# Batch 0 of a fused attention and SwiGLU kernel: turns before scores, idle PSUM banks, and copies split between two engines

## Chip, cores, metric

One core of one Trainium2 chip. The metric is the device time of one execution in microseconds (us); lower is better. Times below are medians of several executions.

## The reference, cut to what matters

Eight batches. Per batch and head: k and v are projected along the sequence by E and F, scores are taken against the projected k, softmax, times the projected v. The result is the input of a gated feed-forward network.

```python
k_proj = np.einsum('ks,bhsd->bhkd', E, k)            # 1024 -> 64 positions
v_proj = np.einsum('ks,bhsd->bhkd', F, v)
scores = scale * np.matmul(q, k_proj.transpose(0, 1, 3, 2))
attn = softmax(scores)                               # max, exp, sum, divide
x = np.matmul(attn, v_proj)                          # then heads side by side
out = (silu(x @ w_gate) * (x @ w_val)) @ w_out       # (8192, 512) x (512, 1536) twice, then back
```

## The kernel before

The main loop runs 192 feature tiles of the feed-forward part, and hides the attention of later batches between them. It cannot start before the first half of batch 0 has gone through attention. This is the stage that the change touches. The pieces, with cuts marked:

```python
ps_g = ... bufs=2   # PSUM: gate        ps_v = ... bufs=2   # value
ps_y = ... bufs=1   # output            ps_a = ... bufs=3   # attention

def u_T(b, u):            # a turn: four transposes of q, then a copy to SBUF
    ps = ps_a.tile([P, 4, P], BF16, name="qTp", tag="pa")
    ...                                      # 4 x nc.tensor.transpose
    nc.scalar.copy(out=t[:], in_=ps[:])
def u_S(b, u):            # scores of one unit, then exp
    ps = ps_a.tile([P, 4, P], FP32, name="sc", tag="pa")
    ...                                      # 4 x nc.tensor.matmul with BD, the projected k
    nc.scalar.activation(out=e, in_=ps, func=AF.Exp, scale=scale)
# u_R: sum and reciprocal on VectorE; u_N: divide (AA); u_A: turn AA, copy to AT;
# u_PV: AT times the projected v (BDV), copy to xT; u_KV: project k or v; u_KT: turn k into BD

turn(0); warm(6)                             # E turned; dummy matmuls that keep TensorE busy
cast_k(nc.vector, 0); cast_k(nc.scalar, 1); cast_k(nc.vector, 2); cast_k(nc.gpsimd, 3)
...                                          # loads of q, v and the first weights
u_KV(0, "k", (0, 4))
cast_k(nc.scalar, 4); cast_k(nc.vector, 5); cast_k(nc.vector, 6); cast_k(nc.scalar, 7)
u_KV(0, "k", (4, 8)); turn(1); u_KT(0)
for u in range(4):
    u_T(0, u); u_S(0, u)
    if u == 1: warm(2)
for u in range(4):
    u_R(0, u); u_N(0, u)
u_A(0, 0); u_A(0, 1); warm(4); u_KV(0, "v", (0, 4))
u_A(0, 2); u_A(0, 3); u_PV(0, 0, 0); u_PV(0, 0, 1); warm(4); u_KV(0, "v", (4, 8))
u_PV(0, 0, 2); u_PV(0, 0, 3)
...                                          # other loads, then the main loop
```

The softmax here doesn't subtract the row's maximum and nothing guards it: scores larger than these inputs give would overflow.

## Time and profile before

| | before |
|---|---|
| median, range of the first 3 runs | 611.54 us, 611.24 to 613.02 us |
| profiled execution | 610.9 us, span on the core 608.7 us |
| TensorE busy | 586.6 us, 96% |
| last quarter of k cast from | 10.56 us |
| fourth exp of batch 0 ends | 22.83 us |
| fourth gate matmul ("start point") | 32.56 us |

Three views matter. The *chain of waits* goes back from the last instruction and names what released each step. The *timeline* has for each group its start, its length, its engine and line, and in brackets how long the engine had been idle and what ended that. The *table by windows* gives busy times and the granted clock per stretch. A group's length tells the clock too: in the traces here eight k or v matmuls of 256 columns took 1.03 to 1.06 us at full clock and 1.86 to 1.92 us at half; four warming matmuls of 512 columns 1.02 to 1.03 and 1.86 to 1.91 us.

### The profile page before, as it was taken

Reading aid. Unit: us, or ns where it says so; the run is one execution under the profiler, and the core shown is the slowest. Engines: PE = TensorE matmul, PEld = TensorE weight load, DVE = VectorE, ACT = ScalarE, POOL = GpSimd, SP = SyncE. Lnnn points to the kernel's source line nnn. Section 1 sums busy time; section 2 is a strip of 40 time slices with the busy share of each in tenths; the row PEclk is TensorE's granted clock in tenths of the full one; section 3 lists DMA queues with packets and bytes.
Section 4 is the critical chain, followed back from the end, with each engine's and each line's share of the span. In section 5 each row is a group of like instructions: output and inputs, shape, how many; then the busy total and the mean of one; then the engine's idle time right before and its main releaser. Section 6 shows DMA issues by size and latency. Waiting matters only on the chain.

```text
span 608.7 us, 8650 instructions
## 1 busy us (share of the span) xinstructions
PE 586.6 (96%) x3279; PEld 289.6 (48%) x3344; DVE 355.7 (58%) x622; ACT 267.0 (44%) x479; POOL 105.7 (17%) x118
## 2 busy tenths in 40 slices
PE   5799999999999999999999999999999999999996
PEld 3444444545544455444544455444554455444443
DVE  3467564756655666556656666656665666655550
ACT  3336344554544445353453445354453544433231
POOL 5615030211300122011310113101220111100000
PEclk9699999999999999999999999999999999999999
DMA  9998963000940039100690009500192000000002
GB/s 227 171 198 136 195 111 70 35 20 34 177 85 34 36 52 206 38 24 28 111 168 18 35 36 154 107 36 36 33 208 56 17 36 36 34 20 36 34 36 86
DMA packets 50681, 48.79 MB, mean 80 GB/s; under 512 B 1872, under 2 KB 41296, under 8 KB 50640
## 3 DMA queue, kind: packets, MB, share of 16 engines
q0 software_dynamic: 40176, 28.84, 32.7%
q1 hardware_dynamic: 10464, 19.40, 8.7%
q8 instruction: 26, 0.43, 0.3%
q14 instruction: 15, 0.12, 0.1%
HBM read 60.29 MB, written 16.78 MB: 127 GB/s over the span
## 4 chain that ended last, share of the span: by engine, by line
PE 93%; ACT 3%; DVE 2%; issue 1%; DMA 1%; another core or an unknown queue 0%; DVEq 0%; ACTq 0%
PE yps L311 27%; PE gps L270 26%; PE vps L285 26%; PE kvp L142 3%; PE sc L201 3%; PE pv L254 2%; PE aTp L241 2%; PE qTp L187 2%; PE warm L409 1%; ACT qT L193 1%; DMA Eraw<-in_E_dram 1%; DVE hT L299 1%; ACT ee L205 0%; ACT ysb L320 0%; ACT xT L261 0%
## 5 line engine op out<-in xcount | busy, mean ns | idle before, releaser
L294 DVE SCALAR_TENSOR_TENSOR s<-th,gps 128x512 f32<-128x512 f32 x192 | 130.4, 679 | 127.9 <-ACT th L278 127.6
L270 PE MATMUL gps<-xT,wg 128*128 128x512 bf16 x761 | 196.9, 379 | 0.8 <-ACT xT L261 0.3
L311 PE MATMUL yps<-wo,hT 128*128 128x512 bf16 x760 | 193.1, 379 | 1.4 <-ACT ysb L320 0.7
L285 PE MATMUL vps<-xT,wv 128*128 128x512 bf16 x720 | 192.2, 379 | 1.9
L278 ACT ACTIVATE th<-gps 128x512 f32<-128x512 f32 x192 | 114.7, 597 | 153.7 <-PE gps L270 124.3
L299 DVE TENSOR_TENSOR hT<-s,vps 128x512 bf16<-128x512 f32 x192 | 131.9, 687 | 22.8 <-PE vps L285 2.5
L224 POOL TENSOR_TENSOR AA<-ee,rr 128x512 bf16<-128x512 f32 x62 | 64.4, 1040 | 417.2 <-DVE rr L218 281.2
L311 PEld LDWEIGHTS <-hT 128*128 128x128 bf16 x768 | 75.2, 98 | 91.4 <-issue 1.0
L270 PEld LDWEIGHTS <-wg 128*128 128x128 bf16 x768 | 72.1, 98 | 76.3 <-issue 1.0
L285 PEld LDWEIGHTS <-wv 128*128 128x128 bf16 x768 | 71.8, 98 | 77.0 <-issue 4.2
L320 ACT ACTIVATE ysb<-yps 128x512 f32<-128x512 f32 x64 | 38.2, 597 | 71.3 <-PE yps L311 68.2
L216 DVE TENSOR_REDUCE zz<-ee 128x8 f32<-128x512 f32 x64 | 43.6, 681 | 18.0 <-ACT ee L205 17.7
L205 ACT ACTIVATE ee<-sc 128x512 f32<-128x512 f32 x64 | 38.2, 596 | 33.7 <-PE sc L201 32.3
L193 ACT COPY qT<-qTp 128x512 bf16<-128x512 bf16 x64 | 37.2, 582 | 25.3 <-PE qTp L187 25.3
L261 ACT CAST xT<-pv 128x512 bf16<-128x512 f32 x64 | 36.8, 582 | 24.0 <-PE pv L254 24.0
L246 DVE COPY AT<-aTp 128x512 bf16<-128x512 bf16 x64 | 26.7, 421 | 22.5 <-PE aTp L241 21.7
L201 PE MATMUL sc<-BD,qT 128*128 128x128 bf16 x256 | 25.5, 224 | 5.2 <-ACT qT L193 4.5
L241 PEld LDWEIGHTS <-AA 128*128 128x128 bf16 x256 | 19.7, 99 | 14.7 <-POOL AA L224 0.4
L187 PEld LDWEIGHTS <-qb 128*128 128x128 bf16 x256 | 19.5, 99 | 13.2 <-issue 1.1
L187 PE MATMUL qTp<-ident_bf,qb 128*128 128x128 bf16 x256 | 25.2, 222 | 0.0
L254 PE MATMUL pv<-AT,BDV 128*128 128x512 bf16 x64 | 23.7, 379 | 1.5 <-DVE AT L246 0.8
L241 PE MATMUL aTp<-ident_bf,AA 128*128 128x128 bf16 x256 | 24.9, 222 | 0.0
(45 smaller groups left out, 175.1 us busy)
## 6 DMA issues: line engine op xcount, KB each, us to landing
out_dram<-ysb SPq DMA_DIRECT2D x64, 256.0 KB, 2.0
qb<-in_q_dram POOLq DMA_DIRECT2D x15, 512.0 KB, 9.5
kb<-in_k_dram POOLq DMA_DIRECT2D x7, 1024.0 KB, 10.7
vb<-in_v_dram POOLq DMA_DIRECT2D x7, 1024.0 KB, 12.4
kraw<-in_k_dram SPq DMA_DIRECT2D x4, 512.0 KB, 5.8
wg<-in_moe_w_gate_dram POOLq DMA_DIRECT2D x6, 256.0 KB, 10.3
wv<-in_moe_w_val_dram POOLq DMA_DIRECT2D x6, 256.0 KB, 10.9
wo<-in_moe_w_out_dram POOLq DMA_DIRECT2D x2, 768.0 KB, 15.8
```

The lines of the kernel that those rows point to most:

```text
L187: nc.tensor.transpose(out=ps[:, n, :], in_=src[:, 4 * g + n, 2 * i : 2 * i + 2, :].rearrange("p j d -> p (j d)"), identity=ident_bf[:],)
L193: nc.scalar.copy(out=t[:], in_=ps[:])
L201: nc.tensor.matmul(out=ps[:, n, :], lhsT=t[:, n, :], rhs=BD[b % 2][:, 4 * g + n, :], start=True, stop=True)
L216: nc.vector.reduce_sum(out=z[:], in_=e[:], axis=AX.X)
L224: eng.tensor_tensor(out=a[:].rearrange("p j h k -> p h j k"), in0=ee.pop((b, u))[:], in1=rr.pop((b, u))[:].unsqueeze(3).to_broadcast([P, 4 ...
L241: nc.tensor.transpose(out=ps[:, pr, j, :], in_=a[:, j, 2 * pr : 2 * pr + 2, :].rearrange("p h k -> p (h k)"), identity=ident_bf[:],)
L270: nc.tensor.matmul(out=ps[:], lhsT=wg[:, kt, f * P : (f + 1) * P], rhs=x[:, kt, :], start=(kt == 0), stop=(kt == NKT - 1),)
L278: nc.scalar.activation(out=th[:], in_=ps[:], func=AF.Tanh, scale=0.5)
L285: nc.tensor.matmul(out=ps[:], lhsT=wv[:, kt, f * P : (f + 1) * P], rhs=x[:, kt, :], start=(kt == 0), stop=(kt == NKT - 1),)
L294: nc.vector.scalar_tensor_tensor(out=s1[:], in0=th[:], scalar=1.0, in1=g[:], op0=ALU.add, op1=ALU.mult)
L299: nc.vector.tensor_tensor(out=hT[c][:, f, :], in0=s1[:], in1=ps[:], op=ALU.mult)
L311: nc.tensor.matmul(out=yy[c][:], lhsT=hT[c][:, f, i * P : (i + 1) * P], rhs=wo[:, f, :], start=(f == 0), stop=(f == NFT - 1),)
```

## The change

The intent: do all turns of q before their scores, so that TensorE does not wait for each copy (in the kernel before it idled 1.76, 0.94, 0.68 and 0.74 us for one ahead of its four score groups); take idle gate, value and output banks so that no tile waits for a bank; share the copies between ScalarE and VectorE; cast k mostly on VectorE; and run the v groups beside the divisions.

```diff
-    def u_T(b, u):
+    def u_T(b, u, at="a", eng=nc.scalar):        # likewise u_S, u_KV, u_KT (at), u_A, u_PV (eng)
...
-            nc.scalar.copy(out=bd[64:128, :, c, 64:128], in_=src)
+            copy(nc.scalar if b else nc.vector, bd[64:128, :, c, 64:128], src)
-        eng = nc.vector if b == 0 and u in (1, 3) else nc.gpsimd
+        eng = nc.vector if b == 0 and u == 3 else nc.gpsimd
...
-        warm(6)
-        cast_k(nc.vector, 0, (0, 8)) ... cast_k(nc.gpsimd, 3, (0, 8))
+        warm(4)
+        for h in range(7):
+            cast_k(nc.gpsimd if h == 3 else nc.vector, h)
...                                     # loads as before
-        u_KV(0, "k", (0, 4)); four casts; u_KV(0, "k", (4, 8)); turn(1); u_KT(0)
-        for u in range(4):
-            u_T(0, u); u_S(0, u)
-            if u == 1: warm(2)
-        for u in range(4):
-            u_R(0, u); u_N(0, u)
-        u_A 0, 1; warm(4); v group; u_A 2, 3; u_PV 0, 1; warm(4); v group; u_PV 2, 3
+        u_KV(0, "k", (0, 4), at="y"); warm(2); cast_k(nc.scalar, 7)
+        u_KV(0, "k", (4, 8), at="y"); turn(1); u_KT(0, at="v")
+        u_T(0, 0, "a", nc.scalar)
+        u_T(0, 1, "a", nc.vector)
+        u_T(0, 2, "a", nc.scalar)
+        u_S(0, 0, "g")
+        u_T(0, 3, "v", nc.vector)
+        u_S(0, 1, "g"); u_S(0, 2, "a"); u_S(0, 3, "a")
+        for u in range(3):
+            u_R(0, u); u_N(0, u)
+        u_KV(0, "v", (0, 4), at="y")
+        u_R(0, 3); u_N(0, 3)
+        u_A(0, 0, nc.scalar); warm(2); u_A(0, 1, nc.scalar)
+        u_KV(0, "v", (4, 8), at="y")
+        u_A(0, 2, nc.scalar); u_PV(0, 0, 0, nc.vector); u_PV(0, 0, 1, nc.vector)
+        u_A(0, 3, nc.scalar); u_PV(0, 0, 2, nc.scalar); u_PV(0, 0, 3, nc.vector)
```

(Several calls per line and words in place of calls are cuts. turn() and warm() also moved to value banks, and turn() copies on ScalarE only.)

More of the change, by code (lines that the diff above doesn't have):

```diff
@@ L130, with bank, copy, u_KV @@
     kvp = {}
-    def u_KV(b, what="kv", hs=(0, H)):
+    banks = {"a": (ps_a, "pa"), "g": (ps_g, "gps"), "v": (ps_v, "vps"), "y": (ps_y, "yps")}
+    def bank(where, shape, dt, name):
+        pool, tag = banks[where]
+        return pool.tile(shape, dt, name=name, tag=tag)
+    def copy(eng, out, in_):
+        (nc.scalar.copy if eng is nc.scalar else eng.tensor_copy)(out=out, in_=in_)
+    def u_KV(b, what="kv", hs=(0, H), at="a"):
         key = (b, what)
         if key not in kvp:
-            kvp[key] = ps_a.tile([P, H, D], FP32, name="kvp", tag="pa")
+            kvp[key] = bank(at, [P, H, D], FP32, "kvp")
         t = kvp[key]
@@ L159, in u_KV, with u_KT @@
             kvp.pop(key)
-    def u_KT(b):
+    def u_KT(b, at="a"):
         ks = kvp.pop((b, "s"))
-        t = ps_a.tile([P, NPAIR, KP], BF16, name="kTp", tag="pa")
+        t = bank(at, [P, NPAIR, KP], BF16, "kTp")
         for pr in range(NPAIR):
@@ L174, in u_KT @@
             nc.vector.tensor_copy(out=bd[0:64, :, c, 0:64], in_=src)
-            nc.scalar.copy(out=bd[64:128, :, c, 64:128], in_=src)
+            copy(nc.scalar if b else nc.vector, bd[64:128, :, c, 64:128], src)
     qT, ee, rr, AA, AT = {}, {}, {}, {}, {}
-    def u_T(b, u):
+    def u_T(b, u, at="a", eng=nc.scalar):
         ch, w = divmod(u, 4)
         g, i = divmod(w, 2)
-        ps = ps_a.tile([P, 4, P], BF16, name="qTp", tag="pa")
+        ps = bank(at, [P, 4, P], BF16, "qTp")
         src = qb[b, ch]
@@ L192, in u_T, with u_S @@
         t = aw.tile([P, 4, P], BF16, name="qT", tag="qT", bufs=4)
-        nc.scalar.copy(out=t[:], in_=ps[:])
+        copy(eng, t[:], ps[:])
         qT[b, u] = t
-    def u_S(b, u):
+    def u_S(b, u, at="a"):
         g = (u % 4) // 2
-        ps = ps_a.tile([P, 4, P], FP32, name="sc", tag="pa")
+        ps = bank(at, [P, 4, P], FP32, "sc")
         t = qT.pop((b, u))
@@ L230, in u_N, with u_A @@
         AA[b, u] = a
-    def u_A(b, u):
+    def u_A(b, u, eng=nc.vector):
         ch, w = divmod(u, 4)
@@ L245, in u_A, with u_PV @@
                 )
-        nc.vector.tensor_copy(
-            out=AT[b, ch][:, 2 * g : 2 * g + 2, 2 * i : 2 * i + 2, :], in_=ps[:]
-        )
-    def u_PV(b, ch, pr):
+        copy(eng, AT[b, ch][:, 2 * g : 2 * g + 2, 2 * i : 2 * i + 2, :], ps[:])
+    def u_PV(b, ch, pr, eng=nc.scalar):
         if (b, ch) not in xT:
@@ L260, in u_PV @@
         )
-        nc.scalar.copy(out=xT[b, ch][:, pr, :], in_=ps[:])
+        copy(eng, xT[b, ch][:, pr, :], ps[:])
     gp = {}
@@ L382, with cast_k @@
         new_k(0)
-        def cast_k(eng, h, js):
-            dst = kb[0][:, h, js[0] : js[1], :].rearrange("p j d -> p (j d)")
-            src = kraw[:, h, js[0] * D : js[1] * D]
-            (nc.scalar.copy if eng is nc.scalar else eng.tensor_copy)(out=dst, in_=src)
+        def cast_k(eng, h):
+            copy(eng, kb[0][:, h].rearrange("p j d -> p (j d)"), kraw[:, h])
         def turn(which):
             for half in range(2):
-                ps = ps_a.tile([P, 4, KP], FP32, name="efp", tag="pa")
+                ps = bank("v", [P, 4, KP], FP32, "efp")
                 for i in range(4):
@@ L399, in turn @@
                 js = slice(4 * half, 4 * half + 4)
-                if half == 0:
-                    nc.vector.tensor_copy(out=(ET, FT)[which][:, js, :], in_=ps[:])
-                else:
-                    nc.scalar.copy(out=(ET, FT)[which][:, js, :], in_=ps[:])
+                copy(nc.scalar, (ET, FT)[which][:, js, :], ps[:])
         def warm(n):
-            ps = ps_y.tile([P, CW], FP32, name="warm", tag="yps")
+            ps = bank("v", [P, CW], FP32, "warm")
             for _ in range(n):
@@ L415 @@
         turn(0)
-        warm(6)
-        cast_k(nc.vector, 0, (0, 8))
-        cast_k(nc.scalar, 1, (0, 8))
-        cast_k(nc.vector, 2, (0, 8))
-        cast_k(nc.gpsimd, 3, (0, 8))
+        warm(4)
+        for h in range(7):
+            cast_k(nc.gpsimd if h == 3 else nc.vector, h)
         load_q(0, 0, 2)
@@ L424 @@
         load_w_gv(1)
-        u_KV(0, "k", (0, 4))
-        cast_k(nc.scalar, 4, (0, 8))
-        cast_k(nc.vector, 5, (0, 8))
-        cast_k(nc.vector, 6, (0, 8))
-        cast_k(nc.scalar, 7, (0, 8))
-        u_KV(0, "k", (4, 8))
-        turn(1)
-        u_KT(0)
-        for u in range(4):
-            u_T(0, u)
-            u_S(0, u)
-            if u == 1:
-                warm(2)
-        for u in range(4):
+        u_KV(0, "k", (0, 4), at="y")
+        warm(2)
+        cast_k(nc.scalar, 7)
+        u_KV(0, "k", (4, 8), at="y")
+        turn(1)
+        u_KT(0, at="v")
+        u_T(0, 0, "a", nc.scalar)
[3 more added lines that the diff above has]
+        u_T(0, 3, "v", nc.vector)
+        u_S(0, 1, "g")
+        u_S(0, 2, "a")
+        u_S(0, 3, "a")
+        for u in range(3):
             u_R(0, u)
             u_N(0, u)
-        u_A(0, 0)
-        u_A(0, 1)
-        warm(4)
-        u_KV(0, "v", (0, 4))
-        u_A(0, 2)
-        u_A(0, 3)
-        u_PV(0, 0, 0)
-        u_PV(0, 0, 1)
-        warm(4)
-        u_KV(0, "v", (4, 8))
-        u_PV(0, 0, 2)
-        u_PV(0, 0, 3)
+        u_KV(0, "v", (0, 4), at="y")
+        u_R(0, 3)
+        u_N(0, 3)
+        u_A(0, 0, nc.scalar)
+        warm(2)
+        u_A(0, 1, nc.scalar)
+        u_KV(0, "v", (4, 8), at="y")
+        u_A(0, 2, nc.scalar)
+        u_PV(0, 0, 0, nc.vector)
+        u_PV(0, 0, 1, nc.vector)
+        u_A(0, 3, nc.scalar)
+        u_PV(0, 0, 2, nc.scalar)
+        u_PV(0, 0, 3, nc.vector)
         load_w_gv(2)
```

## The prediction

> **What bounds the kernel now**
>
> I read the page first (busy shares, slices, chain), then the first 33 us in the chain of waits in order of time, then the timeline of that stretch, then the landing times of the loads.
>
> ```profile
> PE 586.6 (96%) x3279; PEld 289.6 (48%) x3344; DVE 355.7 (58%) x622; ACT 267.0 (44%) x479; POOL 105.7 (17%) x118
> ...
> PE 93%; ACT 3%; DVE 2%; issue 1%; DMA 1%; another core or an unknown queue 0%; DVEq 0%; ACTq 0%
> ```
>
> TensorE is the bound, so the only time to be had lies where it waits. The change touches only work before the main loop and batch 0. The main loop begins with the first gate matmul. In the timeline:
>
> ```profile
> 31.43 1.07 ACT L261 CAST xT<-pv 128x512 bf16<-128x512 f32 x2 [2.20 <-PE pv L254]
> 31.45 1.49 PE L270 MATMUL gps<-xT,wg 128*128 128x512 bf16 x4
> ```
>
> Four xT parts feed the first gate group; the last is copied at 32.5 us, and the fourth gate matmul runs at 32.56 us (chain: "32.56 0.38 PE gps"). I call 32.56 us the start point. After it the chain is nearly all matmuls, spaced by 0.216 us. So the time saved is the distance by which the start point moves, as long as weights and later loads still land in time.
>
> The chain from 13.6 to 24.8 us goes from engine to engine instead:
>
> ```profile
> 13.62 0.29 DVE BD L174
> 13.93 0.37 ACT BD L175
> 14.33 0.30 DVE BD L174
> 14.66 0.37 ACT BD L175
> 15.05 0.59 ACT qT L193
> 15.69 0.41 PE sc L201 x4
> ...
> 19.18 0.59 ACT qT L193
> 19.82 0.62 PE sc L201 x4
> ...
> 21.06 0.48 ACT qT L193
> 21.59 0.61 PE sc L201 x4
> 22.20 0.85 PE aTp L241 x8
> 23.05 1.71 PE warm L409 x4
> 24.76 1.86 PE kvp L142 x8
> ```
>
> The reader is to see a turn of q, a copy on ACT, its scores, and only then the next turn: four rounds of about 1.8 us, since ACT also has an exp of 0.60 us in each round. Then four warming matmuls and the v projection stand in line. At 24.7 us the v data had long landed (below).
>
> Half of this stretch ran at half clock, as the table by windows shows (the third figure from the end of a row is the granted clock):
>
> ```profile
> 16.00:16.25 0.25, 0.25 (x6) 0.13 (x3) 0.00 (x0) 0.13 (x1) 0.00 (x0) 1.00 1.16 160
> 16.25:16.50 0.25, 0.06 (x2) 0.00 (x0) 0.00 (x0) 0.25 (x1) 0.00 (x0) 0.51 1.21 172
> ...
> 26.25:26.50 0.25, 0.25 (x2) 0.00 (x0) 0.00 (x0) 0.00 (x0) 0.25 (x1) 0.51 1.35 170
> 26.50:26.75 0.25, 0.25 (x5) 0.22 (x5) 0.11 (x1) 0.00 (x0) 0.25 (x1) 1.00 1.31 160
> ```
>
> The loads give the floors. Issue time plus time to landing, from the DMA view cut into short windows:
>
> ```profile
> qb<-in_q_dram POOLq DMA_DIRECT2D x1, 256.0 KB, 5.4
> ...
> vb<-in_v_dram POOLq DMA_DIRECT2D x1, 512.0 KB, 8.2
> ...
> vb<-in_v_dram POOLq DMA_DIRECT2D x1, 512.0 KB, 10.0
> ```
>
> Second half of q: issued about 9.05, landed 14.45 us. v: issued 9.88 and 10.6, landed 18.1 and 20.6 us. The first four weight pieces, issued from 11.34 with 10.6 to 12.4 us each, landed at 21.9, 23.3, 24.6 and 25.9 us.
>
> [...]
>
> [...] The trace has 0.588 us for ACT (xT); for DVE its 0.293 us (128 columns) and 0.425 us (256) make 0.69 us by a straight line, which I use. [...] the BD copies on DVE and ACT alternate and never overlap. [...]
>
> **The change part by part**
>
> *k casts.* Before, the last k matmuls started at 11.41, after two ACT casts queued behind the ks copy (10.22 to 11.36). Now only head 7 is on ACT. The last k quarter landed near 10.5 us (the DVE cast that waited for it started at 10.56), so DVE ends head 6 at 10.99 and ACT head 7 at about 11.15: start 11.2. Saved 0.2 us. [...] the second k group may then run cold, 8 x 0.213 us plus latency = 1.85 instead of 1.03 us. That would cost 0.8 us here.
>
> *BD.* Four DVE copies, 4 x 0.31 = 1.24 us, in place of 13.62 to 15.02 = 1.40. With the k gain, BD is ready at 14.65 (or 15.65 if cold) against 15.02.
>
> *Turns first.* In TensorE's order: T0, T1, T2, S0, T3, S1, S2, S3. T2 needs the second half of q, landed 14.45, almost when BD is ready, so it costs nothing. S0 at 14.75, S1 at 15.25 (qT1 copied on DVE, 0.42 us, after BD), S2 at 15.5, S3 at 15.9, done at 16.3. The bank spreading (two score tiles in the gate banks, the fourth turn in a value bank) is what lets this go without waiting for copies. ACT: qT0, qT2 until 15.45, then four exps of 0.60 us: done 16.05, 16.65, 17.25, 17.85. Before, the fourth exp ended at 22.83. So this stage is 5.0 us shorter.
>
> *Normalising.* DVE takes 0.69 + 0.20 us per unit: rr0 16.97, rr1 17.87, rr2 18.78. POOL, now three units instead of two: 17.1 to 18.2, 19.2, 20.25 us. The 0.35 us per unit that POOL is slower matters little, as the next wait is v.
>
> *v.* The first v group cannot start before 18.1. Warm: 18.1 to 19.2; cold 20.0 (1.92 us in the trace). DVE's BDV copies (2 x 0.3 us) stand before unit 3 in its queue: R3 and N3 (0.69 + 0.20 + 0.69 us) end at 21.4 warm, 22.3 cold.
>
> *The tail.* Warm: A0 19.2, A1 20.0, second v group 20.65 (landed 20.6) to 21.7, A2 22.0, BDV 22.3. AT copies on ACT 0.58 each. PV0 and PV1 at 22.0 to 22.6, their xT copies on DVE 0.69 each, 23.1 and 23.8; A3, its copy, PV2 and PV3 run beside them, PV3 done 24.2 and its xT copy at 24.9. Start point 25.0. Cold throughout (matmuls of 128 columns 0.107 us apart, of 512 0.427): A0 20.6, warming 21.3, A1 21.9, second v group 23.65, BDV 24.3, PV1 25.2, xT1 25.8, A3's copy 26.1, PV3 26.9, last xT copy 27.6. Start point 27.65.
>
> *Sum.* 32.56 - 25.0 = 7.5 us at best; 32.56 - 27.65 = 4.9 us at worst. [...] I give the warm course 0.6: 0.6 x 7.5 + 0.4 x 4.9 = 6.5 us. 611.5 - 6.5 = 605.0 us.
>
> **The rivals**
>
> *The weights take the place of the removed waits.* The loads run without a break from 8 to over 50 us (DMA share above 1 in every window), so later weights land when they did before, while the loop wants them up to 7.5 us earlier. For: the loop takes a new piece of the weights every two feature tiles, 3.45 us, and the pieces land only 2.7 us apart or more. Against: each has room. The third pair's value part (issued about 23.95, 5.4 us: 29.3) is wanted at 31.1 or later; q for the second half of the batch (26.14 + 9.5 = 35.6) at 44.86 - 7.6 = 37.2; the fifth pair's value part (27.76 + 10.6 = 38.3) at about 39.5; and k of batch 1 (33.3 + 21.8 = 55.1) at 68.7 - 7.6 = 61.1. The least margin is some 1.2 us. If this rival holds, 1 to 2 us come back: 606 to 607.
>
> *The copies become the bound.* DVE now has the BD, qT, xT copies beside the sums and BDV. [...] the BDV copies, waiting for v, hold up unit 3. For: DVE is busy nearly all of 16 to 24 us in my count. Against: the PV tail hangs on A3 only after PV1's copies. If v were 1 us later, all is 1 us later: 606.
>
> *The clock stays low into the loop.* Only 4 + 2 + 2 = 8 warming matmuls are left of 6 + 2 + 4 + 4 = 16, which gives the array less to do. [...]
>
> *Nothing of it reaches the end.* If the loop had its own slack, the gain would vanish: 611. Against: after 32.56 the chain is TensorE on TensorE.
>
> **Range and chances**
>
> 605.0 us; 8 in 10 between 603.0 and 607.3: from the warm course with the full 7.5 us (604.0) and 1 us of error in my favour, to the cold course (606.6) with 0.7 us against. Faster by over 2% needs 599.3 us, a saving of 12.2 us: the start point would have to be at 20.3, before the second half of v has landed. So faster 0.02, within 2% 0.97, slower 0.01.
>
> **What would show it**
>
> In the timeline of the changed kernel: the fourth gate matmul near 25 to 27.7 us; the four exps back to back and done by 18 to 19 us; the first v group waiting for its DMA at about 18.1 us; the second within 1 us of its landing or right behind A1; the granted clock at 1.00 from 19 us (warm course) or 0.5 until over 22 (cold). The step on the k casts is right if the second k group starts at 11.2. I am wrong if the gate or value matmuls wait for weights between 25 and 45 us, if S2 or S3 waits for a bank, or if the span falls by much less than the start point moves.

The sum came to 32.56 - 25.0 = 7.5 us warm (full clock), 32.56 - 27.65 = 4.9 us cold (half clock), and with the chances of 0.6 and 0.4 to 6.5 us, 605.0 us. The 0.6 and a cold second k group stand as estimates. The spacings at half clock (0.107, 0.213 and 0.427 us for matmuls of 128, 256 and 512 columns) are those of TensorE in the trace of before from 22.2 to 26.2 us. In the profile of before, one unit's division took 1.042 us on GpSimd and 0.691 us on VectorE; the "0.35 us per unit" is their difference. In the changed kernel's profile, VectorE ended the third unit's reciprocal at 21.48 us, then did two BDV copies at 21.52 and 21.82, and only at 22.15 the sum of the fourth unit (R3), whose exp had ended at 20.50.

## The result

| | before | changed |
|---|---|---|
| median, range (4 runs each) | 612.28 us, 611.24 to 613.18 | 605.01 us, 604.50 to 605.28 |
| ratio, 95% interval | | 0.9881, 0.9860 to 0.9902 |
| span of the profiled execution | 608.7 us | 603.5 us |
| start point | 32.56 us | 26.98 us |
| span minus start point | 576.1 us | 576.5 us |

A ratio is the mean time of one kernel's fast runs over that of the other's of the same rounds, so it is not quite the ratio of the medians. The outcome is within 2%, and 605.01 us is next to the predicted 605.0. The page's busy line, and the two lines of the timeline at the start point:

```profile
PE 584.4 (97%) x3272; PEld 288.3 (48%) x3336; DVE 356.8 (59%) x624; ACT 265.8 (44%) x476; POOL 106.7 (18%) x119
```

```profile
26.04 1.32 PE L276 MATMUL gps<-xT,wg 128*128 128x512 bf16 x4
...
26.24 0.69 DVE L138 CAST xT<-pv 128x512 bf16<-128x512 f32 x1 [0.61 <-PE pv L260]
```

The last xT copy, now on VectorE, ends at 26.24 + 0.69 = 26.93 us, and the fourth gate matmul follows at 26.98. TensorE is busy for 2.2 us less in a span that is 5.2 us shorter, so its share rises by a point. The span's 5.2 us are the start point's 5.6 us, less the 0.4 us by which the rest takes longer. That the medians differ by 7.3 us and the profiles by only 5.2 needs an explanation; it is in the next part.

The chain of waits of the changed kernel (start, length, what), where before had four rounds of copy, scores and turn:

```profile
3.00 9.35 DMA kraw<-in_k_dram
...
12.36 0.63 ACT kb L138
...
13.03 1.86 PE kvp L150 x8
...
16.36 1.40 PE qTp L195 x12
17.76 0.43 PE sc L209 x4
18.19 0.43 PE qTp L195 x4
18.62 0.29 PE sc L209 x4
...
18.93 1.09 ACT ee L213 x2
...
20.07 0.68 POOL AA L232
...
21.07 1.04 POOL AA L232
```

Turns and scores now follow one another on TensorE from 16.36 to 18.9 us, and the chain then goes through the exps and GpSimd's divisions. The four exps, which stood in four separate rounds before, now run in one stretch (ScalarE's timeline):

```profile
18.27 2.23 ACT L213 ACTIVATE ee<-sc 128x512 f32<-128x512 f32 x4
```

The first line of the chain is a load: the last quarter of k, issued at 3.00 us, on which everything after it hangs. The timeline, VectorE alone, shows when that quarter could be cast, first in before, then in the changed kernel:

```profile
10.56 0.43 DVE L387 CAST kb<-kraw 128x512 bf16<-128x512 f32 x1 [1.19 <-DMA kraw<-in_k_dram]
```

```profile
12.36 0.51 DVE L138 CAST kb<-kraw 128x512 bf16<-128x512 f32 x1 [0.22 <-DMA kraw<-in_k_dram]
```

In the changed kernel's profiled execution k landed 1.8 us later. Over the 14 profiled executions, of kernels that all issue the k loads in the same way and from 1.4 us on, this moment lay anywhere from 10.47 to 12.81 us. It is not tied to the change: before with some warming matmuls added had 12.51 us. So the profile of before was of a quick execution (610.9 us with a median of 612.3), and a fairer figure for comparing two traces is the *start point minus the cast of the last k*: 22.0 us before, 14.6 us after. That this difference, 7.4 us, is so near the 7.3 us of the medians is partly chance: in the next call the same two kernels are 9.1 us apart by the medians (8.5 us by the ratio).

One thing more differs between executions. The times of before spread from 610.0 to 613.5 us, and the mean granted clock for each execution goes with them. Later, before ran 33 times: the 11 executions with a mean clock of 0.988 to 0.992, as in the profile, took 610.0 to 611.7 us; the other 22, with 0.985 and 0.986 or with 0.999 and 1.000, took 612.3 to 613.5 us. So the profile shows the quicker of two kinds. What the slower kind does in this stage, and whether a late k goes with it, is not known, as no such execution was profiled.

### The profile page after: what moved, and what is told of

It reads as the page before. It is cut to its first block, busy times and chain, and to the rows that moved or that the text cites. A ratio compares the mean times of both kernels' runs of the same rounds, so it can differ in the third digit from the quotient of the medians.

```text
span 603.5 us, 8638 instructions
## 1 busy us (share of the span) xinstructions
PE 584.4 (97%) x3272; PEld 288.3 (48%) x3336; DVE 356.8 (59%) x624; ACT 265.8 (44%) x476; POOL 106.7 (18%) x119
## 4 chain that ended last, share of the span: by engine, by line
PE 93%; ACT 2%; DMA 2%; DVE 1%; issue 1%; SPq 0%; POOL 0%; DVEq 0%; ACTq 0%
PE yps L317 27%; PE vps L291 27%; PE gps L276 26%; PE kvp L150 3%; PE sc L209 2%; PE qTp L195 2%; PE aTp L249 2%; PE pv L260 2%; DMA kraw<-in_k_dram 2%; DVE hT L305 1%; ACT ee L213 0%; ACT qT L138 0%; DVE s L300 0%; DVE zz L224 0%; POOL AA L232 0%
## 5 line engine op out<-in xcount | busy, mean ns | idle before, releaser
L138 ACT CAST xT<-pv 128x512 bf16<-128x512 f32 x61 | 35.3, 582 | 16.9 <-PE pv L260 16.9
L138 DVE COPY AT<-aTp 128x512 bf16<-128x512 bf16 x60 | 25.2, 422 | 22.4 <-PE aTp L249 21.7
L249 PE MATMUL aTp<-ident_bf,AA 128*128 128x128 bf16 x256 | 24.8, 220 | 1.1 <-POOL AA L232 0.8
```

The lines of the kernel that those rows point to most:

```text
L138: (nc.scalar.copy if eng is nc.scalar else eng.tensor_copy)(out=out, in_=in_)
L249: nc.tensor.transpose(out=ps[:, pr, j, :], in_=a[:, j, 2 * pr : 2 * pr + 2, :].rearrange("p h k -> p (h k)"), identity=ident_bf[:],)
```

## The experiments

All were timed in five rounds against before. "k" is the start of the last VectorE cast of k, which waits for its load; "start" is the start of the fourth gate matmul. Both are read from the one profiled execution (in order_undone_filled the record of one of the four gate matmuls is missing; its last one is taken, which follows the one before it by 0.32 us as the fourth does in again). "half clock" is when the array ran at half clock in that execution, by the clock records of its trace and the lengths of the groups.

| run | median us | ratio to before, 95% | k | start | start - k | half clock, us |
|---|---|---|---|---|---|---|
| before | 612.3 to 612.8 | | 10.56 | 32.56 | 22.0 | to 9.4, 16.3-26.5 |
| changed | 605.01 | 0.9881 (0.9860-0.9902) | 12.36 | 26.98 | 14.6 | to 18.6 |
| again | 603.59 | 0.9861 (0.9841-0.9881) | 10.85 | 25.34 | 14.5 | to 12.5 |
| order_undone | 606.74 | 0.9920 (0.9898-0.9942) | 11.36 | 28.98 | 17.6 | to 13.6, 17.0-23.9 |
| tail_undone | 607.94 | 0.9916 (0.9888-0.9945) | 12.81 | 30.89 | 18.1 | to 24.7 |
| copies_undone | 607.13 | 0.9911 (0.9899-0.9923) | 11.83 | 29.05 | 17.2 | to 23.1 |
| banks_undone | 604.96 | 0.9870 (0.9854-0.9886) | 10.47 | 24.98 | 14.5 | to 11.9 |
| casts_undone | 603.75 | 0.9853 (0.9835-0.9871) | 10.77 | 25.37 | 14.6 | to 13.6 |
| order_undone_filled | 607.38 | 0.9910 (0.9893-0.9927) | 11.00 | 27.31 | 16.3 | to 12.5 |
| clock_alone | 611.55 | 0.9985 (0.9966-1.0004) | 12.51 | 34.30 | 21.8 | to 8.0, 11.4-21.7 |
| order_alone | 609.24 | 0.9946 (0.9927-0.9966) | 11.62 | 31.50 | 19.9 | to 23.0 |
| no_warm | 603.81 | 0.9864 (0.9844-0.9884) | 10.54 | 25.16 | 14.6 | to 19.4 |
| better_tail | 603.78 | 0.9860 (0.9839-0.9880) | 11.41 | 25.25 | 13.8 | to 20.1 |
| better_loads | 602.98 | 0.9852 (0.9831-0.9872) | 11.75 | 25.64 | 13.9 | to 20.1 |

In every one of these the span minus the start point is between 576.1 and 576.7 us. So the premise of the whole argument, that the main loop costs the same whenever it starts, held in all fourteen. The last column is a warning: the clock came up for good anywhere from 11.9 us (banks_undone) to 24.7 us (tail_undone) in the changed kernel and its variants, so the difference of one pair of traces holds the edit and the clock together.

Theory: the start point moves, by the order of the score rounds, the copies and the tail, with the clock adding to it. Rivals: the clock alone does it; one part alone does it; the banks or the k casts are main terms.

### again: the changed kernel once more

No edit.

> The changed kernel once more, as the reference for the others. If the saving is the movement of the start point (the fourth gate matmul), the time is 7 us below before (ratio 0.988 to 0.990), and the span minus the start point is 576 to 577 us as in both profiles seen so far. The last quarter of k landed at 10.5 us in the profile of before and at 12.36 us in that of the changed kernel: if that is chance of one execution, here it is somewhere between and the start point moves with it one for one (12.36 gave 26.98, so 10.5 would give about 25.1); if it belongs to the change, it is 12.4 again.

The median was 603.59 us, and k was early (10.85 us) with this same kernel, so its lateness in the first profile was not the change's doing. The start point followed about one for one: 25.34 us, 1.64 us earlier for 1.51 us of k. TensorE's timeline shows what stands next behind k:

```profile
18.03 1.03 PE L150 MATMUL kvp<-vb,FT 128*64 128x256 bf16 x8 [0.94 <-DMA vb<-in_v_dram]
...
20.85 1.06 PE L150 MATMUL kvp<-vb,FT 128*64 128x256 bf16 x8 [0.66 <-DMA vb<-in_v_dram]
```

Both v groups wait for v itself, 0.94 and 0.66 us. With early k the stage, up to the second v group, is at the floor that the loads set; with late k (the first profile) neither v group waits for a load. So the 14.5 and 14.6 us of start minus k come about in two ways. In the first profile the array was at half clock until 18.6 us and the exps ended 8.1 us after k; in again, at full clock, they ended after 7.2 us, and the wait for v took the 0.9 us back. That v is late when k is late has a reason in the traces: GpSimd casts one head of k before it issues the loads of q and v (cast at 7.56 and first issue at 8.37 us in again, 8.66 and 9.47 in the first profile).

### order_undone: turn, scores, turn, scores

```diff
-u_T(0, 0, "a", nc.scalar); u_T(0, 1, "a", nc.vector); u_T(0, 2, "a", nc.scalar); u_S(0, 0, "g")
-u_T(0, 3, "v", nc.vector); u_S(0, 1, "g"); u_S(0, 2, "a"); u_S(0, 3, "a")
+u_T(0, 0, "a", nc.scalar); u_S(0, 0, "g"); u_T(0, 1, "a", nc.vector); u_S(0, 1, "g")
+u_T(0, 2, "a", nc.scalar); u_S(0, 2, "a"); u_T(0, 3, "v", nc.vector); u_S(0, 3, "a")
```

In the diffs that follow T, S, R, N, A and PV with a number stand for these calls for that unit.

> The changed kernel with turns and scores alternating again (T0 S0 T1 S1 T2 S2 T3 S3), all else kept. Theory (the order is a main term): rounds of about 1.25 us (turn 0.4, copy 0.42 or 0.58, scores 0.4) in place of 0.5 us each, so the last scores end 2 us later, the first v group, which stands behind them in TensorE's queue, starts 2 us later: 606.5 to 607.5 us, ratio to before 0.991 to 0.9935. Rival (the banks and the split copies do it, the order is decoration): within 0.5 us of the changed kernel, ratio 0.988 to 0.989.

It measured 606.74 us, 3.1 us over the changed kernel run in the same call, and start minus k grew by 3.1 us. All six executions (606.1 to 609.1 us) lie above the four of again (603.0 to 604.7). The rival falls. TensorE's timeline:

```profile
17.51 0.61 PE L209 MATMUL sc<-BD,qT 128*128 128x128 bf16 x4 [0.52 <-DVE qT L138]
...
19.28 0.61 PE L209 MATMUL sc<-BD,qT 128*128 128x128 bf16 x4 [0.74 <-ACT qT L138]
...
20.84 0.61 PE L209 MATMUL sc<-BD,qT 128*128 128x128 bf16 x4 [0.52 <-DVE qT L138]
21.38 1.92 PE L150 MATMUL kvp<-vb,FT 128*64 128x256 bf16 x8
```

Before each of the last three scores TensorE idles 0.52 to 0.74 us for the copy. The granted clock fell near 17.0 us, as the table by windows shows (0.56 from 17.00 to 17.25, then 0.50 until about 23.8), and the v group that follows runs at half clock, 1.92 us.

### tail_undone: the tail of before

```diff
-R0 N0 R1 N1 R2 N2 | v group | R3 N3 | A0 | warm(2) | A1 | v group | A2 | PV0 PV1 | A3 | PV2 PV3
+R0 N0 ... R3 N3 | A0 A1 | warm(4) | v group | A2 A3 | PV0 PV1 | warm(4) | v group | PV2 PV3
```

(Unit 1 is divided on VectorE again; the copies stay split.)

> The changed kernel with the tail of before (all four sums and divisions, then two A turns, four warming matmuls, v group, two A turns, two PV, four warming matmuls, v group, two PV; unit 1 divided on VectorE), copies still split. Theory: the eight warming matmuls stand in line on TensorE (8 x 0.216 = 1.7 us against 2 x 0.216) and the v groups run after work that waits for the divisions instead of beside it: 2 to 3 us of the 7 come back, 607 to 608 us, ratio 0.991 to 0.9945. Rival (the score rounds alone made the saving, and the tail hides behind v's landing): within 0.6 us of the changed kernel.

It measured 607.94 us, 4.3 us over the changed kernel, and 3.6 us in start minus k: somewhat more than I expected, so in the mean the tail is as large a term as the order. But its six executions run from 604.12, within the changed kernel's range, to 609.48 us, and the array of the profiled one (609.25 us) was at half clock until 24.7 us. How much of the cost is the tail alone, and how much the clock, is not shown. TensorE's timeline shows where the time went, a v group (third line) that starts only behind the divisions and the warming matmuls:

```profile
21.61 1.16 PE L249 MATMUL aTp<-ident_bf,AA 128*128 128x128 bf16 x8 [1.27 <-POOL AA L232]
22.56 1.91 PE L410 MATMUL warm<-BD,ident_bf 128*128 128x512 bf16 x4
24.41 1.17 PE L150 MATMUL kvp<-vb,FT 128*64 128x256 bf16 x8
```

### clock_alone: before with its gaps filled

```diff
 T0
+warm(7)
 S0 T1
-S1 warm(2) T2 S2 T3 S3
+warm(3) S1 T2 warm(3) S2 T3 warm(3) S3
```

> The kernel before with 16 warming matmuls in the gaps of its score rounds in place of 2[...]; nothing else changed. Theory (about 40% of the saving is the clock): the granted clock stays 1.00 from 16 to 27 us, each matmul group on the chain takes 0.4 instead of 0.6 us, the A turns 0.45 less, the v group 0.85 less: 2 to 3.5 us faster than before, ratio 0.994 to 0.997. Rival (waits between engines set the pace and the clock is a symptom): below 0.7 us, ratio 0.999 to 1.0, although the clock reads 1.00.

This failed as a test. In this execution the clock was at half from 11.4 until 21.7 us, so the dummies stood in the way at half rate, and the clock was not up through the stage as the theory asked. TensorE's timeline:

```profile
16.66 3.19 PE L409 MATMUL warm<-BD,ident_bf 128*128 128x512 bf16 x7
```

It measured 611.55 us, 0.15% below before, with an interval that includes no difference. As a test of the time it says nothing for or against the clock's share. It does show that warming matmuls are no safe remedy: seven of them took 3.19 us here.

Other traces say more. The score rounds of the changed kernel ran at half clock in its first profile (but for the last 0.3 us), and so did those of no_warm and better_tail below; start minus k was 14.6, 14.6 and 13.8 us all the same. So the saving does not need a full clock there, and by these traces the clock alone is not the cause. In the tail the clock has a part. From the end of the fourth exp to the start point took 9.7 us in before (half clock until 26.5 us), 8.4 us in this run (full clock all the while) and 6.5 us in the changed kernel's first profile. By these three traces 1.3 of the 3.2 us go with the clock.

### banks_undone, copies_undone, casts_undone: one part each

```diff
 # banks_undone: every T, S, KT, KV and E/F tile of batch 0
-bank(at, ...)  with at = "g", "v", "y" or "a"
+bank("a", ...)                      # warming matmuls in "y"
 # copies_undone
-copies of T1, T3, PV0, PV1, PV3, BD's second half on VectorE; A0 to A3 on ScalarE; E/F on ScalarE
+T, PV, BD's second half on ScalarE; A on VectorE; E/F one half each     (as before)
 # casts_undone
-heads 0, 1, 2, 4, 5, 6 on VectorE, 3 on GpSimd, 7 on ScalarE
+heads 0, 2, 5, 6 on VectorE, 3 on GpSimd, 1, 4, 7 on ScalarE            (as before)
```

> The changed kernel with every tile of the first batch back in the three attention banks (and the warming matmuls in the output bank), order and engines of the copies kept. A tile then waits until the tile three places before it is copied: the third turn waits for the BD copies out of the transposed k, the last scores for the copies of the fourth turn, and the k and v sums hold one of the three banks for long. Theory: 0.5 to 1.5 us slower than the changed kernel run again (603.6), so 604 to 605.2, ratio to before 0.987 to 0.989, and in the trace the third turn starts only after the last BD copy. Rival (banks are half of the saving): 3 us or more, 606.6 and above.

> The changed kernel with each copy of the first batch on its engine of before: all four q copies, the xT copies and half of the BD copies on ScalarE, the AT copies on VectorE. ScalarE then has four copies and four exps, 4 x 0.58 + 4 x 0.60 = 4.7 us, between the turns and the divisions in place of 3.6 us. Theory: the exps end about 1 us later, part of it hidden behind the landing of v; 0.3 to 1.2 us slower than the changed kernel, ratio 0.9865 to 0.9885. Rival (the split is worth nothing, as the chain passes through v): within 0.3 us.

> The changed kernel with the casts of k as before: heads 1, 4 and 7 on ScalarE. Theory of the prediction: 0.2 us on the path, so 603.6 to 604.2 and no difference that five rounds can show (ratio within 0.001 of the changed kernel's). Rival (k casts are a main term, as the change names them): 1 us or more.

*Banks*: 604.96 us, ratio 0.9870; the intervals of this and the changed kernel overlap almost wholly, and start minus k is the same 14.5 us. My reason was partly wrong: the third turn waited 0.28 us for the first q copy and not for the BD copies, so it got another bank than I had counted. The first v group waited 0.91 us, by the trace for the last exp, which ended at 17.72 us; v landed at 17.69, so a wait for a bank, if it was one, cost nothing here. This execution had early k and its second v group waited for v, which can hide a later score round. Whether the banks are worth 1 us in executions with late k stays open; a main term they are not.

*Casts*: 603.75 us, and 14.6 us in start minus k. No effect that shows at the end. Within the stage the second k group started 1.1 us after k in place of 0.7 (and ran at half clock throughout), and the exps ended 8.1 us after k in place of 7.2; the first v group then waited 0.39 us for v in place of 0.94.

*Copies*: 607.13 us, 2.7 us in start minus k over *again*, far above what I expected; its five executions lie within 606.7 and 607.5 us. Two of its lines, from ScalarE's and VectorE's timelines:

```profile
17.35 1.56 ACT L138 COPY qT<-qTp 128x512 bf16<-128x512 bf16 x3
...
19.75 1.63 ACT L213 ACTIVATE ee<-sc 128x512 f32<-128x512 f32 x3
```

```profile
24.03 0.69 DVE L232 TENSOR_TENSOR AA<-ee,rr 128x512 bf16<-128x512 f32 x1
24.75 0.76 DVE L138 COPY AT<-aTp 128x512 bf16<-128x512 bf16 x2
```

ScalarE alone copies the turns and runs the exps, which end at 21.38 us, 9.55 us after k; in *again* they end at 18.09 us, 7.24 after k. Part of this is the clock, at half until 23.1 us here: in the changed kernel's first profile, at half until 18.6, they end 8.1 us after k, so some 1.4 us are left for the copies. Then the first two AT copies stand in VectorE's queue behind the division of unit 3 and run at 24.75 us, although the first A turn was over at 22.95. The change took them off this queue. I had counted only the first of the two effects. The v group ran at half clock here too (1.91 us).

### order_undone_filled: is it the rounds or the clock?

```diff
-T0 S0 T1 S1 T2 S2 T3 S3
+T0 warm(2) S0 T1 warm(2) S1 T2 warm(2) S2 T3 warm(2) S3
```

> Turns and scores alternating, with two warming matmuls in each of the four gaps between a turn and its scores. The gaps were 0.5 to 0.74 us, and two warming matmuls take 0.43 us at full clock and 0.86 at half. In the plain alternating run the clock fell at 17.25 us and came back at 23.9 us, and the v group took 1.92 us against 1.06. Theory (the order costs time in two ways, by the rounds themselves and by letting the clock fall): the clock stays up, the rounds stay near 1.3 to 1.5 us, and 1 to 1.7 us of the 3.1 us that the alternating order cost come back: 605 to 606 us. Rival (it is the rounds alone): 606.5 to 607 us though the clock stays at 1.00. If the clock falls all the same, the run tells neither.

In the profiled execution the clock stayed up, as wanted, and the v group took its 1.06 us:

```profile
19.79 1.06 PE L150 MATMUL kvp<-vb,FT 128*64 128x256 bf16 x8
```

Start minus k was 16.3 us, 1.3 us less than in order_undone, and 1.8 us more than in *again*. By the profiles, then, the 3.1 us of the order split into about 1.8 us of rounds and 1.3 us of clock. The times do not confirm it: the median is 607.38 us against 606.74, with executions from 605.57 (the profiled one) to 608.68. The mean granted clock is 0.999 or 1.000 for all six, so no fall of the clock was recorded in the slower ones. They may have come up from half clock later, which this figure does not count (it is 0.999 for the changed kernel's first profile too); only one was profiled. So the split is what one pair of traces shows and no more.

### order_alone: only the order, in the kernel before

```diff
-for u in range(4): T(u) S(u), warm(2) after u == 1
+T0 T1 T2 S0 T3 S1 S2 S3 warm(2)
```

> The kernel before with only its score rounds reordered: T0 T1 T2 S0 T3 S1 S2 S3, then the two warming matmuls; banks, engines of the copies, casts and tail as before. Theory: ScalarE then runs four q copies and four exps back to back, 4.7 us from 15.05, so the exps end near 19.9 us in place of 22.8; this much shortens the stage, and the tail of before follows unchanged: the start point moves from 22.0 us after the last k landing to 19 to 19.6 us, 2.4 to 3 us faster than before (ratio 0.995 to 0.9965). Rival (without split copies and spread banks the new order gains nothing): below 0.8 us.

609.24 us, ratio 0.9946: 3.3 us faster by the times, 2.1 us in start minus k. The rival falls here as well. With the copies still on ScalarE and the tail as before it is less than half of the 7.4 us. Its exps end 9.8 us after k (before: 12.3), 2.4 us sooner, and 0.3 us of this is given back in the tail. The array was at half clock until 23.0 us here.

### no_warm: without the eight warming matmuls

```diff
-warm(4) ... warm(2) ... warm(2)
```

> The changed kernel without any of its eight warming matmuls. Theory: they stand in gaps and cost nothing[...]; without them the array runs at half clock some microseconds longer, perhaps through the score rounds and the first v group (1.92 us against 1.06): 0.3 to 1.5 us slower than the changed kernel, start point 14.8 to 16 us after the last k landing instead of 14.5. Rival (the second warming group stands in the way of the second k group, and the clock comes up anyway): 0 to 0.4 us faster.

603.81 us and 14.6 us: no difference. The first v group did run partly at half clock (1.65 us), as the theory said, but this did not reach the end: behind it the second A turn waited 0.28 us for GpSimd's division, and the chain of waits goes through the divisions (18.24 to 20.29 us) and not through that v group. The warming matmuls of the changed kernel are not worth anything that these runs can show.

### better_tail and better_loads: a further step

In *again* TensorE waited for ScalarE's AT copies twice in the tail, once because the fourth A turn needed the third one's bank:

```profile
22.92 0.38 PE L249 MATMUL aTp<-ident_bf,AA 128*128 128x128 bf16 x4 [0.24 <-ACT AT L138]
23.97 0.59 PE L260 MATMUL pv<-AT,BDV 128*128 128x512 bf16 x2 [0.67 <-ACT AT L138]
```

```diff
 # better_tail
-A2 (ScalarE) PV0 (VectorE) PV1 (VectorE) A3 (ScalarE) PV2 (ScalarE) PV3 (VectorE)
+A2 (ScalarE) A3 (VectorE, gate bank) PV0 (VectorE) PV1 (ScalarE) PV2 (ScalarE, value bank) PV3 (VectorE, value bank)
 # better_loads: this, and
-cast_k(nc.gpsimd if h == 3 else nc.vector, h)
+cast_k(nc.gpsimd if h == 1 else nc.vector, h)
```

> The changed kernel with its last steps respread: the fourth A turn goes to a gate bank, right after the third and copied by VectorE; the last two PV tiles go to value banks; the four xT copies go to VectorE, ScalarE, ScalarE, VectorE. In both profiles of the changed kernel the fourth A turn waited 0.24 us for the bank that ScalarE's copy of the third held, and the last PV 0.67 us for its own copy. Theory: 0.7 to 0.9 us off the path, start point 13.6 to 13.9 us after the last k landing: 602.7 to 603.2 us against 603.6, 0.0012 to 0.0015 below the changed kernel's ratio. Rival (v's landing and the BDV copies bind): no change, start point at 14.4 or later.

> As better_tail, and GpSimd casts head 1 of k, which lands first, in place of head 3, so that its queue is free to issue the loads of q and v near 6.5 us in place of 8.4 to 9.5 us. Theory: v lands up to 1.5 us earlier and the waits for it go (0.94 and 0.66 us in the run with early k); k is on another queue and lands as before: a further 0.3 to 0.8 us, 602 to 602.8 us. Rival ([...] q's transfers delay the last quarters of k, which the chain needs first): k lands 0.5 to 1.5 us later and the time is that of better_tail or worse.

In better_tail the fourth A turn follows the third without a gap, and so do the four PV:

```profile
22.52 0.77 PE L249 MATMUL aTp<-ident_bf,AA 128*128 128x128 bf16 x8
23.13 1.34 PE L260 MATMUL pv<-AT,BDV 128*128 128x512 bf16 x4
```

Start minus k fell by 0.7 us to 13.8, as expected, but 603.78 us is not below the 603.59 of *again*: a gain of 0.1% is under what five rounds resolve here. better_loads issued q at 6.38 us in place of 8.37, yet v's second half landed at about 20.1 us (its issue plus the 11.1 us to landing) against 20.8 in *again*: 2 us earlier issue, 0.7 us earlier landing. Start minus k stayed at 13.9 us. Its 602.98 us (ratio 0.9852) is the lowest median of all, 1.5% below before; against the changed kernel (ratios 0.9881 and 0.9861) the intervals overlap, so that it beats it is not shown.

## Why the prediction was right, point by point

- **The start point moves and the loop follows.** Right: 576.1 to 576.7 us after the start point in fourteen profiles. No gate or value matmul of the first tiles waited for weights, so the first rival fell.
- **The score stage, 5.0 us shorter.** Right at full clock. From the k cast to the end of the fourth exp: 12.27 us before, 7.24 us in *again* (predicted 7.35). In the changed kernel's first profile, at half clock until 18.6 us, it was 8.1, so 4.1 us shorter. BD took 1.21 us (predicted 1.24).
- **v as the next floor.** Right with early k: first v group at 18.03 (predicted 18.1), second at 20.85 (20.65). With late k it was GpSimd's divisions that set the second group's time, by way of the second A turn: TensorE waited 0.64 us for the first and 0.17 us for the second division. That GpSimd's 1.04 us for a division, against VectorE's 0.69, matters little, as the prediction says, did not hold there.
- **The tail.** The warm course gave a start point of 25.0 us; *again* has 25.34. The tail costs 3.6 us when undone, with the clock in it, so the later part of the stage had as much to give as the score rounds named in the title of the change.
- **k casts.** Predicted 0.2 us, possibly lost to a cold second k group. The second k group did run at half clock (1.48 to 1.86 us in place of 1.03) and started at 11.52 us in *again*, not at 11.2; undoing the casts shows nothing in the time.
- **The clock.** Here a term was mis-sized. I gave the cold course a chance of 0.4, which cut the saving from 7.5 to 6.5 us. In both profiles of the changed kernel the clock was up for the v groups and the tail, and the saving was 7.3 us and 8.5. That the time met 605.0 to 0.01 us is luck: the saving was 0.8 us above the 6.5 forecast, and the new rounds had before at 612.28, 0.7 us above the three runs that I had started from.
- **Readings and sums.** Two are off, and neither moves the result. "Half of this stretch" at half clock is three quarters: 16.25 to 24.8 us of 13.6 to 24.8. BD "at 15.65 if cold" is 15.45 by the prediction's own 0.8 us. The straight line's 0.69 us for a VectorE copy of 512 fp32 columns was right: the xT copy took 0.69 us in the changed kernel (0.59 on ScalarE).
- **What I did not see** was the 2 us by which the k load varies from one execution to the next, and that before has a quicker and a slower kind of execution. My start from the profile of before took an early k and the quicker kind for the rule.

Undone one at a time, order, tail and copies cost 3.1, 3.6 and 2.7 us: 9.4 us of a 7.4 us saving. They are not independent: in all three profiles the array was at half clock up to the first v group or through it, whereas in *again* it was at full clock from 12.5 us; and each undoing puts work on the chain behind something new. So the three figures show that each part counts, and not how the 7.4 us divide.

## What to carry to other kernels

When a stage goes engine to engine, put the instructions of one engine in the order in which their inputs become ready, not in the order of the data flow (undoing this cost 3.1 us here, the clock included), and look in each engine's timeline for a copy that ran only after work it does not need (in copies_undone the first AT copies ran at 24.75 us, behind a division, for a turn that was over at 22.95). Look at when the clock came up in each trace before comparing two of them (from 11.9 to 24.7 us in the changed kernel and its variants). Measure such a stage from the load that starts it, since a load that varies by 2 us (k could be cast at 10.47 to 12.81 us in 14 profiles) hides a 1 us change in the whole time. Dummy matmuls for the clock were not free when the clock was down (seven took 3.19 us in clock_alone), and in the changed kernel leaving out all eight made no difference.
